# Windowed attention and an ELU feed-forward network in fp32 on one core: softmax spread over the blocks around it, one PSUM copy moved to VectorE, masks between transposes

## The chip, the cores and the metric

One core of one Trainium2 chip. The metric is the device time of one execution in microseconds. The core has TensorE (PE; PEld is its weight load), VectorE (DVE), ScalarE (ACT), GpSimd (POOL) and SyncE (SP, which issues the transfers here).

## The reference

```python
def _attn_ref(q, k, v):              # 8 batches, 8 heads, 576 positions, 64 wide
    scores = np.matmul(q, k.transpose(0, 1, 3, 2)) / np.sqrt(D)
    rel = pos[:, None] - pos[None, :]
    mask_plain = (rel >= 0) & (rel < 32)                      # heads 0 to 3
    mask_dil = (rel >= 0) & (rel < 128) & (rel % 4 == 0)      # heads 4 to 7
    scores = np.where(masks, scores, -1e9)
    scores = scores - scores.max(-1)
    attn = np.exp(scores); attn = attn / (attn.sum(-1) + 1e-9)
    return np.matmul(attn, v)

def _moe_ref(x, w_in, w_out):        # x: 4608 x 512, w_in: 512 x 2048, w_out: 2048 x 512
    h = x @ w_in
    g = np.where(h > 0, h, np.exp(np.minimum(h, 0)) - 1)
    return g @ w_out
```

The attention's result, with the heads side by side, is the x of the feed-forward network.

## The kernel before

The 4608 tokens are cut into 9 chunks of 512, the 8 batches have 576 tokens each. The attention of batch b has to be ready before the chunks that hold its tokens, so it is done in pieces between the matmuls of earlier chunks. Matmuls in fp32 accuracy are made of three passes over a rounded value (`h`, `gh`, `xh`: a cast on ScalarE) and its residual (`l`, `gl`, `xl`: a subtraction on VectorE).

**Chunks 0 to 2** loop over 16 blocks `f` of 128 hidden columns. A block is one first product (12 matmuls of 512 columns), the ELU (`elu`: ScalarE copies the PSUM tile, exponential, relu; VectorE combines; ScalarE casts `gh`; VectorE subtracts `gl`), and the second product of the block two before it (`flush`, 12 matmuls of 512 columns). `elu` is a generator: its tail, cast and `gl`, is run within the next block's `elu`, after that one's copy of the PSUM tile. In chunk 2's last blocks the tail runs at once. In chunks 1 and 2 weight blocks are also split (`split_late`, L180 and L182) and combined for the later chunks (`combine`, L230 to L237, in the blocks that `COMBINE` names).

**Chunks 3 to 8** (`combined_chunk`) replace the first product of 2 x 2 blocks by seven products of sums of blocks (`ORDER`), in four groups `g` of seven steps `s`. Each step is a product (12 matmuls of 256 columns), then what `TODO[s]` lists for ScalarE and VectorE, operand casts and residuals (`moving_operand`, listed in `OPERANDS`; `rest:B22` is the residual of operand B22), and some second products from a queue (`pop`). `work(spare)`, the entries `w0` to `w6`, takes softmax steps from the list `side` up to a budget of `SPARE[g][s]`.

**The attention pieces.** A scores piece (`scores_piece`, two head pairs, 144 small matmuls) uses three PSUM banks: the two `a_ps` and `h1`, shown as `h`. After a third of it, a one-column copy into `nothing` (L481) reads the third bank, so that the last third of the matmuls, which writes this bank for the second head, comes after it. Then the masks are added from PSUM into `sm` (VectorE), maximum, subtraction, exponential (ScalarE), sum, normalisation and six 32-row transposes into `pt`, for each head pair. An output piece (`outputs_piece`, 48 matmuls) needs both pairs' transposes. For batches 2 and 3 (`b <= CS`), the scores pieces stand in chunk 1, blocks 0 and 7, and in chunk 2, blocks 1 and 7, the output pieces in blocks 6 and 13 and in blocks 6 and 12 (`WHEN`), and all of the softmax is written right after the scores. For batches 4 to 7 `later_probabilities` adds the masks at once and puts the rest on `side`; batch 4's first piece stands in chunk 2, block 14, the others in chunks 3 to 6, at steps 9 and 23 of the 28 (`PIECES`). There are two `sm` buffers: a tile `sm` and a part of `a5` (shown as `a`). At step 9 the list `side` is emptied before the piece (`work(100.0)`).

**What sets the order.** All matmuls, and every operation given to `vec` and `act`, are pinned: each stands on its engine's queue behind the operation that was written before it. Other operations of VectorE and ScalarE (`nc.vector`, `nc.scalar`) are ordered by a planner, which runs the program in a simulated time and takes what is ready, the earlier written first. In chunks 1 and 2 the ELU and softmax are of this kind, until chunk 2's block 14 (`LAST`), from where all are pinned.

Of the kernel before, what the change touches and what calls it, by code (L numbers as in the profile page):

```python
# [24 lines left out]
G = 32  # L25
# [18 lines left out]
CS = 3  # L44
# [7 lines left out]
SPARE = ((0.9, 0.3, 1.0, 0.9, 1.2, 2.2, 0.3), (0.9, 0.9, 0.0, 1.6, 2.2, 1.0, 0.3), (0.9, 0.9, 2.2, 1.2, 2.0, 2.4, 0.3), (0.6, 0.6, 0.0, 0.3, 0.6, 1.2, 0.3))  # L52
OPERANDS = [t.split() for t in ("", "cast:B11 make:T1", "rest:B11", "make:T2 cast:T2", "rest:T2", "make:T3", "cast:T3 rest:T3",
                                "cast:B21 rest:B21", "make:T4 cast:T1", "rest:T1 cast:T4", "rest:T4 cast:B22", "rest:B22", "", "")]
WHEN = {1: (0, 6, 7, 13), 2: (1, 6, 7, 12)}
EARLY = 0.0
LAST = 14
OPER = 12
PLAIN = ("a5", "a-1'")
COMBINE = {(1, 11): 0, (1, 13): 1, (1, 15): 2, (2, 1): 3, (2, 4): 4, (2, 6): 5, (2, 9): 6, (2, 11): 7}  # L60
PIECES = {9: ("S", 2, 1), 14: ("O", 0, 1), 21: ("O", 2, 1), 23: ("S", 0, 2)}

TINY = float(np.array([0x38000000], np.uint32).view(np.float32)[0])
# [3 lines left out]
def body(ctx: ExitStack, tc: tile.TileContext, q, k, v, masks, w_in, w_out, out):  # L67
# [235 lines left out]
    def normalise(eng, sm, sums, keep):  # L303
        keep(nc.vector.tensor_scalar(out=sums, in0=sums, scalar1=1e-9, scalar2=None, op0=ALU.add))
        keep(nc.vector.reciprocal(out=sums, in_=sums))
        return keep(eng.tensor_tensor(out=sm, in0=sm, in1=sums.unsqueeze(2).broadcast_to([QB, 2 * NU, 2 * G]), op=ALU.mult))

    def transposed():
        count[0] += 1
        return pt[count[0] % len(pt)]  # L310
# [89 lines left out]
    def probabilities(b, hp, sm, nmx, sums):  # L400
# [10 lines left out]
                last_transpose[b] = nc.vector.transpose(out=tr[ks, :, cs], in_=sm[cs, :, rs]).ins  # L411
        return b, hp, tr

    def three():

        return banks() + [ps_h.tile([P, TC], F32, name="h1")]
# [9 lines left out]
    vec, act = Ordered(nc.vector), Ordered(nc.scalar)  # L426
    side, held = [], []

    def work(spare):

        while side and spare > 0:
            cost, step = side.pop(0)
            step()
            spare -= cost

    def later_probabilities(b, hps, groups):

        other_sm = slots("a5", 2, 3).rearrange("p o t -> p (o t)")[:QB, :2 * NU * 2 * G].rearrange("p (u j) -> p u j", u=2 * NU)
        sms = [ap.tile([QB, 2 * NU, 2 * G], F32, name="sm", bufs=1), other_sm]
        for j in (1, 0):  # L440
            masks_added(hps[j], groups[j], sms[j], vec)
        small = [[ap.tile([QB, 2 * NU], F32, name=n, bufs=4) for n in ("nmx", "sums")] for _ in hps]
        trs = [transposed() for _ in hps]
        wide = lambda x: x.unsqueeze(2).broadcast_to([QB, 2 * NU, 2 * G])

        def steps(j):

            sm, (mx, sums), tr = sms[j], small[j], trs[j]
            yield 0.9, lambda: vec.tensor_reduce(out=mx, in_=sm, op=ALU.max, axis=mybir.AxisListType.X)
            yield 0.9, lambda: vec.tensor_tensor(out=sm, in0=sm, in1=wide(mx), op=ALU.subtract)  # L450
            yield 0.0, lambda: act.activation(out=sm, in_=sm, func=AF.Exp, scale=0.125)
            yield 0.9, lambda: vec.tensor_reduce(out=sums, in_=sm, op=ALU.add, axis=mybir.AxisListType.X)
            yield 0.1, lambda: vec.tensor_scalar(out=sums, in0=sums, scalar1=1e-9, scalar2=None, op0=ALU.add)
            yield 0.1, lambda: vec.reciprocal(out=sums, in_=sums)
            yield 0.9, lambda: vec.tensor_tensor(out=sm, in0=sm, in1=wide(sums), op=ALU.mult)
            for c in range(GU):
                for r in range(2):
                    ks, cs, rs = slice((c + r) * G, (c + r + 1) * G), slice(c * G, (c + 1) * G), slice(r * G, (r + 1) * G)
                    yield 0.57, lambda ks=ks, cs=cs, rs=rs: vec.transpose(out=tr[ks, :, cs], in_=sm[cs, :, rs])

        one, other = list(steps(0)), list(steps(1))
        side.extend([*one[:2], other[0], one[2], other[1], one[3], other[2], *one[4:7], *other[3:7]])
        (held if hps[0] else side).extend(one[7:] + other[7:])
        return [(b, hp, tr) for hp, tr in zip(hps, trs)]

    def scores_piece(b, hps):

        s = three()

        def place(j, h, n0, n1):  # L470

            bank, o = (s[h], n0 + j * NU) if j == 0 or n0 < 2 else (s[2], n0 - 2 + h * 4)
            return bank[:, o * 2 * G:(o + n1 - n0) * 2 * G]

        qk = [qk_of.pop(b * NPAIR + hp) for hp in hps]

        one, other = [(0, n) for n in range(NU)], [(1, n) for n in range(NU)]
        for i, (first_head, second_head) in enumerate(zip(other[2:] + other[:2] + one, other[:2] + one + other[2:])):
            if i == 4:

                nc.scalar.copy(out=nothing, in_=place(1, 0, NU - 1, NU)[:QB, 2 * G - 1:])  # L481
            for c in range(GU):
                for h, (j, n) in enumerate((first_head, second_head)):
                    score(place(j, h, n, n + 1), *qk[j], h, n, c)
        groups = [[[(n0, n1, place(j, h, n0, n1)) for n0, n1 in (((0, NU),), ((2, NU), (0, 2)))[j]] for h in range(2)] for j in range(2)]
        if b <= CS:
            made = [probabilities(*exponentials(b, hp, groups[j])) for j, hp in enumerate(hps)]
        else:
            made = later_probabilities(b, hps, groups)
        for hp in hps:  # L490
            load_qk(b * NPAIR + hp + 2)
        return made
# [238 lines left out]
    def combined_chunk(c):  # L731

        x_ps = y_ps = None
        halves = lambda x: x.rearrange("p (i t) -> p i t", i=2)
        for g in range(NG):
            base = (c - CS) * NG * 7 + g * 7
            for s in range(7):
                step = 7 * g + s
                what, hp, ahead = PIECES.get(step, ("", 0, B))
                if what and c + ahead < B:  # L740
                    if what == "S":
                        if hp:
                            work(100.0)
                        made[hp] = scores_piece(c + ahead, (hp, hp + 1))
                    else:
                        if hp:
                            work(100.0)
                        outputs_piece(made.pop(hp))
                        if hp == 0:
                            side.extend(held)  # L750
                            held.clear()
                load_combined(base + s + RING)
                if s == 0:
                    x_ps = ps_h.tile([P, TC], F32, name="h0")
                    live["before"], live["now"] = live.get("now"), (c, g, [sets.pop(0), sets.pop(0)])
                    sets.extend(live["now"][2])
                if (c, g, s) == (CS, 1, 0):
                    moving["temporary"] = late
                if s == 3:
                    y_ps = ps_h.tile([P, TC], F32, name="h1")  # L760
                product(base + s, x_ps if ORDER[s] in ("A11", "S2", "S3", "A22") else y_ps, s in (0, 3, 4))
                for what in TODO[s]:
                    if what in ("u1", "u2", "u3"):
                        live[what] = fp.tile([P, TC], F32, name="e")
                        act.copy(out=live[what], in_=x_ps)
                    elif what == "C21":
                        act.copy(out=rows[1][:, :, :HT], in_=halves(x_ps))
                    elif what[0] == "C":
                        to, u = {"C11": (rows[0][:, :, :HT], "u1"), "C22": (rows[1][:, :, HT:], "u3"), "C12": (rows[0][:, :, HT:], "u2")}[what]
                        vec.tensor_tensor(out=to, in0=halves(y_ps), in1=halves(live.pop(u)), op=ALU.add)  # L770
                    elif what[0] == "w":
                        work(SPARE[g][s])
                    elif what[0] == "p":
                        push(int(what[4:]))
                    else:
                        activation(what)
                if g == NG - 1 and c + 1 < NCH:
                    for what in OPERANDS[s]:
                        moving_operand(c + 1, what, vec, act)
                if g == 0:  # L780
                    for what in OPERANDS[7 + s]:
                        moving_operand(c, what, vec, act)
                pop((FIRST_POPS if (c, g) == (CS, 0) else POPS)[s])
# [83 lines left out]
    for c in range(CS):  # L867
# [14 lines left out]
        for f in range(NF):  # L882
# [29 lines left out]
            else:  # L912
                steps = elu(gemm1(c, f), c, f, before, *strict)
                g = next(steps)
                if c == 0 or c == CS - 1 and f >= NF - 3:
                    if g[1] is not None:
                        next(steps)
                    steps = None
                before = steps
                pend.append((c, f, g))  # L920
            if c == 1:
                keep_plain(f)
            if (c, f) == (0, 0):
# [103 lines left out]
```

## Time and profile before

| | |
|---|---|
| median of 3 runs | 884.86 us (884.64 to 887.34) |
| profiled execution | 884.33 us, span 882.5 us |
| TensorE clock granted, mean | 0.994 |
| PE busy | 863.4 us, 98% of the span |
| VectorE busy | 609.1 us, 69% |
| ScalarE busy | 455.7 us, 52% |
| chunk 2 (230 to 328 us) | VectorE busy 80.04 of 98.00 us |
| DMA | 170.68 MB, mean 193 GB/s |

The span runs from the first to the last instruction. In rows of the timeline the first number is the start in us from the span's beginning, the second the length, then engine, line, operation, output and inputs, shapes and count, and in brackets the engine's idle time before it and what ended that. The line is that of a helper for many: L104 is every matmul, L424 every pinned operation. In the list of waits, the numbers are total us, times, and the longest.

### The profile page before, as it was taken

What the parts mean: (1) busy time and instruction counts of PE and PEld (TensorE: products, weight loads), DVE (VectorE), ACT (ScalarE), POOL (GpSimd) and SP (SyncE); (2) the same over time, 40 slices, a digit from 0 to 9 for tenths busy, and PEclk for the clock granted to TensorE, in tenths of its full rate; (3) what the DMA queues carried; (4) which work ended last, traced back from release to release, by engine and by line L of the source; (5) the groups of instructions that cost most, each with busy time, mean ns of one, the idle gap of its engine ahead of it and who ended that gap; (6) DMA issues with size and microseconds to landing.
All of it is one profiled execution on the core that took longest, in us unless ns stands there. A gap on an engine that the chain in (4) does not pass through costs nothing. (4 is left out here: it accounts for less than half of the span.)

```text
span 882.5 us, 17850 instructions
## 1 busy us (share of the span) xinstructions
PE 863.4 (98%) x7424; PEld 725.6 (82%) x7424; DVE 609.1 (69%) x921; ACT 455.7 (52%) x783; POOL 6.0 (1%) x12
## 2 busy tenths in 40 slices
PE   6999999999999999999999999999999999999998
PEld 5545678878878888898989998889898989998996
DVE  6999998867588968966867597748775533453332
ACT  3666667645655565434554455446454453454334
POOL 2000000000000000000000000000000000000000
PEclk7999999999999999999999999999999999999999
DMA  9996335123454657757575657656665565557541
GB/s 342 387 356 245 123 121 187 48 92 120 155 199 156 198 165 226 227 187 236 176 258 188 225 178 248 219 182 223 196 199 167 167 215 176 183 175 224 175 144 48
DMA packets 66961, 170.68 MB, mean 193 GB/s; under 512 B 6752, under 2 KB 21440, under 8 KB 66880
## 3 DMA queue, kind: packets, MB, share of 16 engines
q1 hardware_dynamic: 66880, 169.54, 58.9%
q8 instruction: 59, 0.97, 0.4%
q14 instruction: 22, 0.18, 0.1%
HBM read 141.20 MB, written 28.31 MB: 192 GB/s over the span
## 5 line engine op out<-in xcount | busy, mean ns | idle before, releaser
L104 PE MATMUL h<-xh,r 128*128 128x256 f32 (+1 forms) x984 | 223.2, 308 | 2.1 <-PE h L104 1.0
L104 PEld LDWEIGHTS h<-xh,r 128*128 128x128 f32 x984 | 165.1, 191 | 13.9 <-PE h L104 1.2
L104 PE MATMUL h<-xl,r 128*128 128x256 f32 (+1 forms) x492 | 142.7, 307 | 0.6 <-DVE xl L424 0.6
L104 PE MATMUL o_ps<-a,r 128*128 128x512 f32 x480 | 117.0, 391 | 0.0
L424 DVE SCALAR_TENSOR_TENSOR a-1_3249<-a-1_3249,a 128x1024 f32<-128x1024 f32 x48 | 58.7, 1223 | 83.2 <-ACT a L424 83.1
L424 DVE TENSOR_TENSOR a-1_3249<-h,e 128x512 f32<-128x512 f32 x72 | 49.7, 690 | 82.5 <-PE h L104 81.1
L104 PEld LDWEIGHTS h<-xl,r 128*128 128x128 f32 x492 | 93.8, 191 | 9.0 <-issue 2.1
L104 PEld LDWEIGHTS o_ps<-a,r 128*128 128x128 f32 x480 | 87.6, 188 | 16.5
L104 PE MATMUL o_ps<-a,gh 128*128 128x512 f32 x248 | 89.4, 463 | 0.0
L424 ACT COPY e<-h 128x512 f32<-128x512 f32 x72 | 42.2, 586 | 80.8 <-PE h L104 65.7
L104 PE MATMUL h<-a,r 128*128 128x256 f32 x576 | 77.5, 284 | 0.0
L104 PEld LDWEIGHTS h<-a,r 128*128 128x128 f32 x576 | 74.0, 191 | 3.0
L424 ACT COPY a-1_3249<-h 128x512 f32<-128x512 f32 x24 | 14.1, 587 | 109.6 <-PE h L104 109.6
L104 PEld LDWEIGHTS o_ps<-a,gh 128*128 128x128 f32 x248 | 46.3, 188 | 24.2 <-issue 17.2
L424 ACT ACTIVATE a<-a 128x1024 f32<-128x1024 f32 (+1 forms) x56 | 57.0, 1030 | 1.3
L104 PE MATMUL o_ps<-r,r 128*128 128x512 f32 x212 | 56.8, 391 | 0.0
L104 PE MATMUL o_ps<-a,a 128*128 128x512 f32 x216 | 54.6, 391 | 0.0
L424 ACT ACTIVATE a<-a-1_3249 128x1024 f32<-128x1024 f32 x48 | 51.0, 1063 | 1.3 <-DVE a-1_3249 L424 0.5
L104 PEld LDWEIGHTS o_ps<-a,a 128*128 128x128 f32 x216 | 39.4, 188 | 7.4
L424 ACT CAST r<-a-1_3249 128x1024 fp32r<-128x1024 f32 x32 | 33.6, 1050 | 22.2 <-DVE a-1_3249 L424 22.1
L104 PEld LDWEIGHTS o_ps<-r,r 128*128 128x128 f32 x212 | 38.7, 188 | 7.3
L424 DVE TENSOR_TENSOR r<-a-1_3249,r 128x1024 fp32r<-128x1024 f32 x32 | 39.0, 1218 | 6.7 <-ACT r L424 6.2
(179 smaller groups left out, 1431.6 us busy)
## 6 DMA issues: line engine op xcount, KB each, us to landing
r<-combined SPq DMA_DIRECT2D x168, 512.0 KB, 4.1
vt<-v SPq DMA_DIRECT2D x30, 384.0 KB, 4.2
kt<-k SPq DMA_DIRECT2D x30, 304.0 KB, 4.9
out<-e SPq DMA_DIRECT2D x35, 256.0 KB, 3.1
qt<-q SPq DMA_DIRECT2D x30, 288.0 KB, 4.0
r<-w_in SPq DMA_DIRECT2D x16, 512.0 KB, 7.6
r<-w_out SPq DMA_DIRECT2D x16, 512.0 KB, 8.0
combined<-a SPq DMA_DIRECT2D x20, 256.0 KB, 2.9
```

The lines of the kernel that those rows point to most:

```text
L104: return inorder(nc.tensor.matmul(*args, **kw))
L424: return lambda *args, **kw: inorder(getattr(self.eng, name)(*args, **kw))
```

## The change

Six edits:

1. The first scores piece of chunk 2 goes from block 1 to block 2; its output piece stays in block 6.
2. For batches 2 and 3 the softmax is a generator, `softmax`. The first head pair's masks to normalisation are written at the scores; then, one entry of `spread` in each of the next four blocks, right after the block's ELU: three transposes of the first pair; its other three, and the second pair's masks to normalisation; three transposes of the second pair; its last three.
3. In blocks that hold an attention piece (`f in when`), the tail of this block's ELU (cast and `gl`) is written at once, ahead of the piece.
4. For batches 4 to 7 the one-column copy is a pinned VectorE operation.
5. In chunk 3, step 9, `work(100.0, LEFT)` leaves three transposes on `side`. `later_probabilities` then swaps the two `sm` buffers, adds the second pair's masks, does the three transposes, adds the first pair's masks, and lets the second pair go first in the steps that follow. With an empty list the order is the one before.
6. In chunk 3, group 0, step 4, `rest:B22` is written ahead of the step's list.

```diff
-WHEN = {1: (0, 6, 7, 13), 2: (1, 6, 7, 12)}
+WHEN = {1: (0, 6, 7, 13), 2: (2, 6, 7, 12)}
+LEFT = 3
...
+    spread = []
+    def softmax(b, hp, places, tr):
+        _, _, sm, _, sums = exponentials(b, hp, places)
+        normalise(nc.vector, sm, sums, lambda ins: ins)
+        yield
+        for c in range(GU):
+            for r in range(2):
+                ks, cs, rs = slice((c + r) * G, (c + r + 1) * G), slice(c * G, (c + 1) * G), slice(r * G, (r + 1) * G)
+                last_transpose[b] = nc.vector.transpose(out=tr[ks, :, cs], in_=sm[cs, :, rs]).ins
+                if (c, r) == (1, 0):
+                    yield
+        yield
...
-    def work(spare):
-        while side and spare > 0:
+    def work(spare, left=0):
+        while len(side) > left and spare > 0:
...
@@ later_probabilities @@
-        for j in (1, 0):
-            masks_added(hps[j], groups[j], sms[j], vec)
+        one, other = (1, 0) if side else (0, 1)
+        if side:
+            sms.reverse()
+        masks_added(hps[1], groups[1], sms[1], vec)
+        work(100.0)
+        masks_added(hps[0], groups[0], sms[0], vec)
...
-        one, other = list(steps(0)), list(steps(1))
+        one, other = list(steps(one)), list(steps(other))
...
@@ scores_piece @@
-                nc.scalar.copy(out=nothing, in_=place(1, 0, NU - 1, NU)[:QB, 2 * G - 1:])
+                (vec.tensor_copy if b > CS else nc.scalar.copy)(out=nothing, in_=place(1, 0, NU - 1, NU)[:QB, 2 * G - 1:])
...
-            made = [probabilities(*exponentials(b, hp, groups[j])) for j, hp in enumerate(hps)]
+            trs = [transposed() for _ in hps]
+            made = [(b, hp, tr) for hp, tr in zip(hps, trs)]
+            one, other = [softmax(b, hp, groups[j], trs[j]) for j, hp in enumerate(hps)]
+            next(one)
+            spread.extend(((one,), (one, other), (other,), (other,)))
...
@@ combined_chunk @@
-                            work(100.0)
+                            work(100.0, LEFT if c == CS else 0)
...
+                if (c, g, s) == (CS, 0, 4):
+                    moving_operand(c, *OPERANDS[7 + s], vec, act)
...
-                if g == 0:
+                if g == 0 and (c, s) != (CS, 4):
...
@@ the loop over blocks @@
+                if steps is not None and f in when:
+                    next(steps)
+                    steps = None
                 before = steps
                 pend.append((c, f, g))
+            for steps in spread.pop(0) if spread else ():
+                next(steps)
```

## Prediction

> **What bounds the kernel now.** I read the page first, then the waits of PE, then stretches of the timeline around each wait, engine by engine.
>
> ```profile
> span 882.5 us, 17850 instructions
> PE 863.4 (98%) x7424; PEld 725.6 (82%) x7424; DVE 609.1 (69%) x921; ACT 455.7 (52%) x783; POOL 6.0 (1%) x12
> ...
> q8 instruction: 59, 0.97, 0.4%
> ...
> PE h L104 <- issue: 0.9, 1, 0.9
> ```
>
> PE is busy 98% and the change alters no matmul. So only PE's holes can be won, and any new wait of PE is lost one for one. I price a hole by starts: from the last matmul before it to the first after it, less the usual distance (0.23 us at 512 columns, 0.12 at 256). The last line, from the list of PE's waits, is one in which it waits for nothing that the profile shows. Seven holes after 130 us are over 0.4 us. The change reaches all of them, and opens others.
>
> **The change part by part.** *Softmax of chunks 1 and 2 in pieces.* In the kernel before, both head pairs' softmax is written where the scores are, so in the written order it stands ahead of the residual `gl` of the block before:
>
> ```profile
> 183.87 0.69 DVE L573 SCALAR_TENSOR_TENSOR e<-h,e 128x512 f32<-128x512 f32 x1 [0.42 <-ACT e L572]
> 184.37 0.15 ACT L481 COPY nothing<-h 96x1 f32<-96x1 f32 x1 [0.54 <-PE h L104]
> 191.21 3.48 DVE L411 STREAM_TRANSPOSE pt<-sm 32x384 f32<-32x384 f32 x6
> 194.73 0.69 DVE L578 TENSOR_TENSOR gl<-e,gh 128x512 fp32r<-128x512 f32 x1
> 193.56 0.61 PE L104 MATMUL o_ps<-a,gh 128*128 128x512 f32 x2
> 195.47 0.50 PE L104 MATMUL o_ps<-a,gl 128*128 128x512 f32 x1 [1.29 <-DVE gl L578]
> ```
>
> `gl` could have followed the activation of 183.87; it ran 10 us later, behind six transposes. The second matmul of the pair began at 193.56 + 0.61 - 0.39 = 193.78, so the hole is 195.47 - 193.78 - 0.23 = **1.46**. The edit writes `gl` ahead of the scores and halves the transposes: I take the whole 1.46 as won (between 1.0 and 1.46; a block of three transposes, 1.74 us, is the longest it can still meet).
>
> *The piece of chunk 2 goes from block 1 to block 2.* Soon after the scores at 243.9 PE stops in the middle of a product for which nothing is outstanding:
>
> ```profile
> 243.90 0.24 PE L104 MATMUL h<-kt,qt 64*32 64x64 f32 x1
> ...
> 245.63 0.50 PE L104 MATMUL h<-xh,r 128*128 128x512 f32 x1
> ...
> 246.89 0.40 PE L104 MATMUL h<-xl,r 128*128 128x512 f32 x1
> 248.24 0.39 PE L104 MATMUL h<-xh,r 128*128 128x512 f32 x1 [0.95 <-issue]
> ...
> 248.53 1.18 ACT L236 CAST e<-a 128x512 fp32r<-128x512 f32 x2 [1.80 <-DMA out<-e]
> 249.80 0.59 ACT L558 COPY h<-h 128x512 f32<-128x512 f32 x1
> 249.18 1.29 DVE L237 TENSOR_TENSOR a<-a,e 128x512 fp32r<-128x512 f32 x2 [3.24 <-ACT e L236]
> 250.39 0.55 DVE L375 TENSOR_TENSOR sm<-a_ps,masks_sb 96x384 f32<-96x384 f32 x1
> ```
>
> That hole is 1.35 - 0.23 = **1.12**. The page's instruction queue moved 59 packets of 0.97 MB together, 16.4 KB each, for PE's 7424 matmuls and as many weight loads: some 252 instructions a packet. A scores piece is 144 matmuls with 144 loads in 245.63 - 243.90 = 1.7 us, more than one packet, so I read the stop as PE waiting for instructions. One block later the piece begins 48 instructions (24 matmuls and loads) further on against the packets, and of the eleven other pieces, which begin elsewhere against them, none is followed by such a row. I take the 1.12 as won (0 to 1.12). [...]
>
> The same rows show what the piece moves into. ScalarE is held until 248.53 by the stores of chunk 0's and 1's results. The copy of block 2's hidden tile comes at 249.80, and behind it a cast, an exponential and a relu of about 0.6 each (that copy's and the casts' time): to 252.1. The scores now begin one block later, 243.9 + 24 x 0.227 = 249.35, and their last third, 0.6 long, needs ScalarE's one-column copy (`nothing`) at 249.35 + 1.7 - 0.6 = 250.4. If that copy queues behind the three, PE waits 1.7; if it also queues behind the cast of block 2, which is now written ahead of the scores, 3.0; if the planner slips it in, 0. I take **1.3** lost (0 to 3.0), nearer to the first, since what is written first and ready goes first.
>
> *The outputs of that piece keep their place (block 6), so softmax has one block less.*
>
> ```profile
> 269.86 3.48 DVE L411 STREAM_TRANSPOSE pt<-sm 32x384 f32<-32x384 f32 x6
> 273.37 1.29 DVE L237 TENSOR_TENSOR a<-a,e 128x512 fp32r<-128x512 f32 x2
> 274.58 1.29 DVE L573 SCALAR_TENSOR_TENSOR e<-h,e 128x512 f32<-128x512 f32 x2
> ...
> 274.52 0.39 PE L104 MATMUL a_ps<-pt,vt 128*64 128x96 f32 x4
> ```
>
> VectorE needed 250.39 to 273.34, 22.95 us, from the second half of the first mask add to the last transpose; the outputs began 1.2 us after. With the change the masks start at the end of the scores, 250.9, with both halves to do (0.5 more): 250.9 + 0.5 + 22.95 = 274.35 at best. The outputs begin at 274.52 - 1.12 = 273.4 and come to the second pair's transposes halfway, at 274.35. But the last three transposes are now written at block 6, behind the two L237, the activation of block 5 and its `gl` (each 1.29 for two): 1.2 + 0.6 + 0.6 = 2.4 us more, and perhaps block 6's own pair, 1.2. Lost 0 to 3.6; the wait at 250.4 would let VectorE do some of this meanwhile. I take **2.0**.
>
> *Cast and `gl` ahead of the other pieces, and smaller holes under 0.2.* At 184.37 the copy ran before the cast was ready (the activation ended at 184.56); with the cast first it would end at 184.56 + 0.6 + 0.15 = 185.3 instead of 184.5, a little after which PE needs it. Net **0.2** lost (0 to 0.8).
>
> *The one-column copy goes from ScalarE to VectorE for batches 4 to 7*, pinned behind what VectorE was given before it. In chunks 4 and 6:
>
> ```profile
> 448.99 0.49 PE L104 MATMUL a_ps<-kt,qt 64*32 64x64 f32 x26
> 450.39 0.24 PE L104 MATMUL h<-kt,qt 64*32 64x64 f32 x1 [0.92 <-ACT nothing L481]
> 451.22 0.75 DVE L424 TENSOR_TENSOR a<-h,masks_sb 96x256 f32<-96x256 f32 x2 [4.36 <-PE h L104]
> 635.82 0.24 PE L104 MATMUL h<-kt,qt 64*32 64x64 f32 x1 [0.40 <-ACT nothing L481]
> ```
>
> Holes: 450.39 - (448.99 + 0.49 - 0.22) = **1.13**, 0.21 over the idle time that the row gives, and so 0.40 + 0.21 = **0.61** in chunk 6. VectorE sits idle there (4.36 before the masks), so both go. No row shows this copy on VectorE; between 0 and the 0.37 of one mask add (two in 0.75) I take 0.15, ScalarE's own time for it (184.37). It is done in time with either.
>
> But batch 4's first piece stands in chunk 2's block 14, where every operation is pinned:
>
> ```profile
> 322.66 0.46 PE L104 MATMUL a_ps<-kt,qt 64*32 64x64 f32 x23
> 323.35 0.24 PE L104 MATMUL h<-kt,qt 64*32 64x64 f32 x1 [0.23 <-ACT nothing L481]
> 323.94 0.69 DVE L424 SCALAR_TENSOR_TENSOR e<-h,e 128x512 f32<-128x512 f32 x1 [2.29 <-ACT e L424]
> 325.32 0.69 DVE L424 TENSOR_TENSOR r<-e,gh 128x512 fp32r<-128x512 f32 x1 [0.69 <-ACT gh L424]
> 325.93 0.74 DVE L424 TENSOR_TENSOR a<-h,masks_sb 96x256 f32<-96x256 f32 x2
> ```
>
> There VectorE waits for the relu, then for the cast, and the mask adds come only at 325.93. The copy now stands right ahead of them: 325.93 + 0.15 and 0.05 to PE's start, and PE goes on at 326.13 instead of 323.35. That is **2.78 lost**, where a free VectorE would have won the 0.45 of this hole (323.35 less 322.66 + 0.46 - 0.24, and the piece's own step). No later slack takes it back: the next hidden product follows on PE, and the VectorE operations after the masks wait for that product in turn. Ends: 2.6 and 3.0 by the price of the copy.
>
> *Chunk 3: `rest:B22` first, masks between the transposes.*
>
> ```profile
> 340.46 0.69 DVE L424 TENSOR_TENSOR a-1_3249<-h,e 128x512 f32<-128x512 f32 x1 [0.68 <-PE h L104]
> 343.26 0.68 DVE L424 TENSOR_TENSOR xl<-x,xh 128x512 fp32r<-128x512 f32 x1
> 343.08 0.28 PE L104 MATMUL h<-xh,r 128*128 128x256 f32 x1
> 343.99 0.39 PE L104 MATMUL h<-xl,r 128*128 128x256 f32 x1 [0.63 <-DVE xl L424]
> 354.39 3.48 DVE L424 STREAM_TRANSPOSE pt<-a 32x384 f32<-32x384 f32 x6
> 358.00 0.75 DVE L424 TENSOR_TENSOR a<-h,masks_sb 96x256 f32<-96x256 f32 x2
> 356.15 1.70 PE L104 MATMUL h<-r,r 128*128 128x256 f32 x12
> 358.86 0.36 PE L104 MATMUL h<-xh,r 128*128 128x256 f32 x1 [1.01 <-PE h L104]
> ```
>
> The residual of 343.26 moves ahead of 340.46, into 0.68 us of idle time: hole 343.99 - 343.08 - 0.12 = **0.79** gone. The second hole, 358.86 - (356.15 + 1.70 - 0.28) - 0.12 = **1.17**, is PE waiting for the bank `h` that the two mask adds of 358.00 release; they stand behind seven transposes of 0.58, one and the six of 354.39. Three now come after: the adds could start 1.7 us earlier. But the copy on VectorE also stands behind the four that stay: 354.39 + 3 x 0.58 = 356.13, where PE wants it for the last third of the scores, 0.6 before the product of 356.15, at 355.55 less the 0.79 just won. So a new wait of up to 1.5 opens inside the scores, 0.8 if VectorE's chain, which starts from PE's results, moves up by 0.7 with PE. Of 0.79 + 1.17 = 1.96 I take 1.96 - 0.85 = **1.1** won (0.45 to 1.96).
>
> **The sum.** Won: 1.46 + 1.12 + 1.13 + 0.61 + 1.1 = 5.42. Lost: 2.78 + 1.3 + 2.0 + 0.2 = 6.28. Net +0.86 on the profiled execution's 884.33 (span 882.5 and 1.8 around it): 885.2. The median of the runs, 884.86, is 0.53 above that execution, so **885.7** in their terms. What a measurement can tell from no change is about 0.3%, 2.65 us: 882.2 to 887.5.
>
> **The rivals.** *The planner lets the early pieces through.* ScalarE's copy at block 2 goes ahead of the backlog and the transposes run before L237: 1.3 + 2.0 + 0.2 not lost, 885.7 - 3.5 = 882.2. For it: VectorE and ScalarE outside pinned stretches are ordered by readiness (the L237 pair at 249.18 cut between two halves of a mask add). Against: where several were ready at once, as from 273.37 on, they ran in written order. Chance 0.18; half of it beyond 0.3%.
>
> *The copy at block 14 is not held* (it would have to run before the `gl` of 325.32): 885.7 - 2.78 - 0.45 = 882.5. Only a wrong reading of the pinning allows it. Chance 0.08.
>
> *Slower: the cast ahead of the one-column copy on ScalarE.* At all four pieces of chunks 1 and 2 the cast now stands first in written order.
>
> ```profile
> 141.93 0.69 DVE L573 SCALAR_TENSOR_TENSOR e<-h,e 128x512 f32<-128x512 f32 x1 [0.39 <-ACT nothing L481]
> ```
>
> At block 0 of chunk 1 the copy would end at 141.93 + 0.69 + 0.6 + 0.15 = 143.4 instead of 141.9: 1.5. Block 7 costs 0.6, block 2 of chunk 2 3.0, its last piece some 0.2: 5.3 where the sum has 1.5, so 889.5. It decides the sign when the four pass 3.3 together. For it: written order won from 273.37 on. Against: at 184.37 the copy was ready first. Chance 0.22.
>
> *The stop at 246.89 is no fetch and stays:* 886.8, within the band; chance 0.1, which I leave in the forecast's.
>
> **How the numbers follow.** The forecast has 0.52, the rivals 0.18, 0.08 and 0.22. Faster by over 0.3%: 0.09 + 0.05 and a little for both of the first two together: 0.16. Slower: 0.22 and 0.04 from the forecast's upper end: 0.26. The rest, 0.58, is within. The forecast's own range is 883.0 to 888.0; for 8 in 10 it goes from 881.8 (first rival, a little beyond) to 888.8 (most of the third).
>
> **What would show it.** No wait of PE for L578 `gl` near 194; no issue gap after the scores of chunk 2; a wait of PE near 323 of about 3.2 us, for VectorE's `nothing`; no wait for `xl` near 343, and near 355 one for `nothing` instead of 1.0 before 358.86; none near 449 and 635. The unsure ones: PE for ScalarE's `nothing` near 250, and for `pt` near 274. I am wrong if the piece at block 14 runs through, or if those two are near 0 or near their upper ends.

## Result and profile after

The changed kernel takes 892.79 us (median, 891.02 to 894.61) against 885.69 (884.64 to 887.34) for the kernel before in the same runs: a ratio of 1.0081, 95% interval 1.0064 to 1.0098. It is 7.1 us slower; the forecast was 885.7 in a range of 881.8 to 888.8. The profiled execution took 892.01 us, 7.68 more than the one of before (884.33).

From the page of the kernel after, and the top of PE's list of waits from 130 us on (total, times, longest):

```profile
span 890.2 us, 17851 instructions
PE 865.8 (97%) x7424; PEld 726.6 (82%) x7424; DVE 611.9 (69%) x929; ACT 455.4 (51%) x775; POOL 6.0 (1%) x12
...
PE h L105 <- DVE nothing L440: 4.4, 2, 3.0
PE h L105 <- ACT nothing L501: 2.3, 2, 1.5
PE h L105 <- ACT h L582: 1.5, 1, 1.5
PE o_ps L105 <- DVE gl L602: 0.7, 1, 0.7
PE a_ps L105 <- DVE pt L425: 0.6, 1, 0.6
```

The first, second and fifth were in the prediction. The fourth is not the wait for `gl` that was to go, but one for the `gl` of the next block. The third was not foreseen: PE waits for ScalarE's copy of a hidden tile out of its bank `h`. These are its rows (ScalarE, then VectorE, then PE):

```profile
141.96 0.62 ACT L601 CAST gh<-e 128x512 fp32r<-128x512 f32 x1
148.51 0.84 ACT L397 ACTIVATE sm<-sm 96x768 f32<-96x768 f32 x1 [4.03 <-DVE sm L396]
149.26 0.56 ACT L582 COPY h<-h 128x512 f32<-128x512 f32 x1
...
142.62 0.69 DVE L602 TENSOR_TENSOR gl<-e,gh 128x512 fp32r<-128x512 f32 x1 [0.69 <-ACT gh L601]
143.22 0.55 DVE L376 TENSOR_TENSOR sm<-a_ps,masks_sb 96x384 f32<-96x384 f32 x1
143.69 2.35 DVE L183 TENSOR_TENSOR a<-a,a 128x1024 fp32r<-128x1024 f32 x2
145.96 0.55 DVE L376 TENSOR_TENSOR sm<-a_ps,masks_sb 96x384 f32<-96x384 f32 x1
...
148.00 0.39 PE L105 MATMUL o_ps<-r,gl 128*128 128x512 f32 x1
149.88 0.50 PE L105 MATMUL h<-xh,r 128*128 128x512 f32 x1 [1.49 <-ACT h L582]
```

The cast and `gl` run ahead of the mask adds. Between PE's scores and the second mask add now stand `gl` (0.60 us) and two adds of L183 (2.27 us), which split a weight block. In the kernel before the same two adds run at 140.32 and 152.86. They are tied to `gl` in the code: `split_late` stands under `issue_after(low[-1])` and `issue_after(high[-1])`, behind the last `gl` and cast that were written. With the tail of block 0 written at once, that is block 0's for both, so one add is held back until then and the other is let go early; that is read from the code, and the times of both kernels fit it. ScalarE's exponential therefore gets its operand at 148.49. The copy of `h` stands behind it on ScalarE's queue and does not pass it, though ScalarE idles for 4.03 us and the last matmul of the product to be copied began before 145.5. In the kernel before, the same exponential had run 3 us earlier, at 145.55, the copy at 146.31, and PE went on without a hole:

```profile
145.55 0.85 ACT L396 ACTIVATE sm<-sm 96x768 f32<-96x768 f32 x1 [3.62 <-DVE sm L395]
146.31 0.57 ACT L558 COPY h<-h 128x512 f32<-128x512 f32 x1
...
148.22 0.39 PE L104 MATMUL h<-xh,r 128*128 128x512 f32 x1
```

The hole, by starts, is 149.88 - 148.00 - 0.23 = 1.65 us. At block 14 of chunk 2 (VectorE's rows), and then in the busy time by stretches (PE, PEld, VectorE, ScalarE, GpSimd, then the granted clock):

```profile
328.39 0.69 DVE L440 SCALAR_TENSOR_TENSOR e<-h,e 128x512 f32<-128x512 f32 x1 [2.29 <-ACT e L440]
329.77 0.69 DVE L440 TENSOR_TENSOR r<-e,gh 128x512 fp32r<-128x512 f32 x1 [0.68 <-ACT gh L440]
330.38 0.15 DVE L440 COPY nothing<-h 96x1 f32<-96x1 f32 x1
...
318.00:325.00 7.00, 7.00 (x33) 5.80 (x32) 5.17 (x13) 5.10 (x12) 0.00 (x0) 1.00 0.61 198
329.50:336.30 6.80, 5.72 (x57) 4.59 (x58) 2.83 (x8) 0.23 (x1) 0.00 (x0) 0.50 0.48 157
336.30:343.00 6.70, 6.70 (x42) 5.96 (x42) 3.54 (x6) 4.13 (x9) 0.00 (x0) 1.00 0.31 100
```

The copy stands where the prediction put it, right behind the `gl` of that block. It takes 0.15 us, as estimated. PE's hole is 3.22 us; the one of before was 0.44, so the hold costs 2.78. What was not foreseen is the second row of the stretches: with the hold, TensorE drops to half clock for 6.83 us. The scores of block 14 began 4.44 us later than before, those of chunk 3 8.85 us. Of the 4.41 between them, 2.78 are the hold and 0.79 the `xl` hole, won back; 2.42 are left over, which I put down to the half clock.

The other pieces. Around 195 and 201 the order of VectorE and what PE does, at block 2 of chunk 2 the order of ScalarE, and near 364 that of VectorE again:

```profile
185.84 0.69 DVE L602 TENSOR_TENSOR gl<-e,gh 128x512 fp32r<-128x512 f32 x1 [0.68 <-PE h L105]
195.84 0.39 PE L105 MATMUL o_ps<-a,gl 128*128 128x512 f32 x1
...
194.29 3.48 DVE L425 STREAM_TRANSPOSE pt<-sm 32x384 f32<-32x384 f32 x6
197.81 0.69 DVE L597 SCALAR_TENSOR_TENSOR e<-h,e 128x512 f32<-128x512 f32 x1
201.45 0.68 DVE L602 TENSOR_TENSOR gl<-e,gh 128x512 fp32r<-128x512 f32 x1
202.19 0.50 PE L105 MATMUL o_ps<-a,gl 128*128 128x512 f32 x1 [0.75 <-DVE gl L602]
...
253.03 0.62 ACT L601 CAST gh<-e 128x512 fp32r<-128x512 f32 x1 [0.76 <-DVE e L597]
253.56 0.15 ACT L501 COPY nothing<-h 96x1 f32<-96x1 f32 x1
...
363.46 0.57 DVE L440 STREAM_TRANSPOSE pt<-sm 32x384 f32<-32x384 f32 x1
364.06 1.73 DVE L440 STREAM_TRANSPOSE pt<-a 32x384 f32<-32x384 f32 x3
365.82 0.15 DVE L440 COPY nothing<-h 96x1 f32<-96x1 f32 x1
```

The `gl` that had stopped PE at 193.8 in the kernel before ran at 185.84, and the matmul that reads it ran at 195.84 without a hole. But the six transposes, written in halves, still ran as one block of 3.48 us, ahead of the next block's activation (197.81), though its relu had ended at 193.62. That block's `gl` came only at 201.45, behind the transposes and the mask adds, maximum and subtraction of the other head pair: a new hole of 0.91. At block 2 the one-column copy ran behind the cast, as in the prediction's upper case; here that cost 1.67 us. Near 364 it ran behind four transposes: 1.61 us.

### The profile page after: what moved, and what is told of

It reads as the page before. It is cut to its first block, busy times and chain, and to the rows that moved or that the text cites. A ratio compares the mean times of both kernels' runs of the same rounds, so it can differ in the third digit from the quotient of the medians.

```text
span 890.2 us, 17851 instructions
## 1 busy us (share of the span) xinstructions
PE 865.8 (97%) x7424; PEld 726.6 (82%) x7424; DVE 611.9 (69%) x929; ACT 455.4 (51%) x775; POOL 6.0 (1%) x12
## 4 chain that ended last, share of the span: by engine, by line
PE 79%; DVE 12%; ACT 4%; issue 2%; DMA 1%; POOL 0%; SPq 0%; DVEq 0%; ACTq 0%
PE h L105 38%; PE o_ps L105 37%; PE a_ps L105 4%; DVE pt L425 2%; DMA out<-e 1%; DVE nmx L389 1%; DVE sm L376 1%; DVE e L597 1%; DVE sm L307 1%; DVE gl L602 1%; DVE sm L396 1%; DVE a L183 0%; ACT pt L362 0%; DMA kt<-k 0%; DVE sums L398 0%
```

## Experiments

Each median is beside that of the kernel before in runs on the same chip: 885.2 us for the first four, 884.97 for the next four, 884.36 for the last four. Holes are start to start, less the usual distance, as in the prediction.

**One part undone, one part alone: the copy at block 14.** First from the kernel after, then from the kernel before.

```diff
-                (vec.tensor_copy if b > CS else nc.scalar.copy)(...)
+                (vec.tensor_copy if b > CS and (b > CS + 1 or hps[0] > 0) else nc.scalar.copy)(...)
```

> The changed kernel, with the one-column copy of batch 4's first piece (chunk 2, block 14) back on ScalarE and nothing else undone. Theory A: the hold of 3.2 us there costs 2.8 us itself and, by setting the granted clock to one half for 6.8 us behind it, about 2.4 us more. Then this run takes 892.8 - 5.2 = 887.6, the products after the piece start 0.23 us apart and the mean granted clock is near 0.995. Rival B: the half clock has nothing to do with the hold. Then 890.0, with the clock still near 0.992.

Measured 889.17 us, ratio 1.0041 (1.0027 to 1.0055), 3.5 us below the kernel after (0.0081 - 0.0041 of 885). That lies between the two figures expected, and fits neither. The hold at block 14 is gone. But in its profiled execution ScalarE's copy at block 2 held PE for 3.49 us instead of 1.67, and 3.41 us of half clock followed there.

```diff
-                nc.scalar.copy(...)
+                (vec.tensor_copy if b == CS + 1 and hps[0] == 0 else nc.scalar.copy)(...)
```

> The kernel before, with only the one-column copy of batch 4's first piece moved to VectorE, behind what VectorE holds there. Theory A: 885.7 + 2.8 + 2.4 = 890.9, with a stretch of half clock behind the piece. Rival B: 888.5 at an undisturbed clock. Rival C: something later takes the hold back, 886 or less.

Measured 888.52 us, ratio 1.0039 (1.0026 to 1.0053): 3.3 us lost by one copy of 0.15 us. Its hole is 3.22 us, as in the kernel after. Here the profile shows full clock behind it:

```profile
PE h L105 <- DVE nothing L440: 3.0, 1, 3.0
...
326.50:333.30 6.80, 6.80 (x79) 5.89 (x80) 2.77 (x7) 2.34 (x4) 0.00 (x0) 1.00 0.53 178
```

**The late edits alone, and the early edits alone.** The first is the kernel before with only what concerns batches 5 to 7 and chunk 3: the copy on VectorE for `b > CS + 1`, mask adds between transposes, `rest:B22` first. The second has only the edits of chunks 1 and 2: the piece at block 2, softmax spread, cast and `gl` ahead; all copies stay on ScalarE.

> The kernel before, with the edits of chunks 3 to 6 alone: rest:B22 early, masks between transposes at chunk 3's step 9, the copy on VectorE for batches 5 to 7 only (batch 4 keeps it on ScalarE). Theory A: the four holes close, 0.79 + 1.17 + 1.13 + 0.61 = 3.7, so 882.0. Rival B: VectorE's chain is the next limit in chunk 3, so the 0.79 and 1.17 come back as another wait there; 884.0.

Measured 882.95 us, ratio 0.9972 (0.9960 to 0.9983): faster than both kernels. The holes at 343, 449 and 635 are gone. In place of the 1.17 us at 357.6 there is one of 1.06, with no releaser, shown below; so the gain is between the two figures expected.

> The kernel before, with the edits of chunks 1 and 2 alone: softmax in pieces, the scores piece in block 2, cast and residual ahead of the pieces; the copy stays on ScalarE everywhere, chunk 3 as before. Theory A: the waits that the changed kernel's trace shows before chunk 2's block 14 are due to these edits, net 4.1 us at that point (326.34 - 321.90 less 0.3 that the two runs differ at the start): 889.8. Rival B: as predicted for these terms, 1.46 + 1.12 won, 3.5 lost: 886.6.

Measured 890.41 us, ratio 1.0059 (1.0040 to 1.0077). So the early edits, priced at 3.5 lost against 2.58 won, lose 5.2 us, close to theory A. In this profile the wait for ScalarE's copies is the longest, 3.53 us by starts at block 2:

```profile
PE h L105 <- ACT nothing L501: 4.1, 2, 3.3
...
252.54 0.63 ACT L587 ACTIVATE e<-h 128x512 f32<-128x512 f32 x1 [2.12 <-DMA out<-e]
```

The second row shows why it is longer here than in the kernel after: ahead of the cast and the copy, ScalarE's exponential waits 2.12 us for a store of results (2.09 in the profile with 3.49 us), where it waits 0.17 in the profile of the kernel after.

**The three early edits, each alone.**

```diff
-WHEN = {1: (0, 6, 7, 13), 2: (1, 6, 7, 12)}
+WHEN = {1: (0, 6, 7, 13), 2: (2, 6, 7, 12)}
```

> The kernel before with only the first scores piece of chunk 2 put at block 2 instead of block 1. By the prediction's terms the stop of 1.12 us at 246.9 goes and ScalarE's copy `nothing` costs 1.3 us: 885.2 + 0.2 = 885.4 us. Rival, from the profile after: the copy waits behind the exponential and the cast of gh, PE holds for 1.67 us (3.5 us where the copy is the later one), and the stop of 1.12 us came in only some executions, so that nothing is won by losing it: 886.9 to 888.7 us.

Measured 885.64 us, ratio 1.0009 (1.0000 to 1.0018): close to no change. That is near the 885.4 expected, but by other terms: the copy is not held by itself (its hole at block 2 is 0.22 us), no stop follows the scores, and the outputs wait 1.43 us at 275.

> The kernel before with only the probabilities of the pieces of chunks 1 and 2 spread over the blocks that follow. By the prediction's terms the hole of 1.45 us at 193.8 goes and 0.2 us is lost to casts: 885.2 - 1.3 = 883.9 us. Rival, from the profile after: the hole keeps 0.91 us, PE waits 1.65 us at 148 for ScalarE's copy of h that is queued behind the exponential, and 0.3 to 1.0 us each at 186, 215 and 286: 885.2 - 0.54 + 1.65 + 0.29 + 0.31 + 1.01 = 887.9 us.

Its edit is the one of `scores_piece` in the diff above (`softmax`, `spread`). Measured 884.30 us, ratio 0.9994 (0.9985 to 1.0004): no change that can be told. No hole at 148; 0.87 us are left of the one at 194, so the median is near the 883.9 expected without the gain that was to bring it there.

```diff
+                if steps is not None and f in when:
+                    next(steps)
+                    steps = None
```

> The kernel before with only the second output step put one block earlier where a scores piece stands. The prediction's 2.0 us came from transposes that are spread; without the spread they are over when the outputs begin, so no change: 885.2 us, within 0.6. Rival: the outputs wait for pt as they do in the profile after (0.22 and 0.80 us), whether the transposes are spread or not: 886.2 us.

That text names the edit wrongly: what these lines move is the cast to `gh` and `gl` of a block, ahead of the piece, and no output step. Both its prices fall. Measured 889.22 us, ratio 1.0040 (1.0027 to 1.0053): this edit alone loses 4.25 us. Its waits between 130 and 300 us:

```profile
PE o_ps L105 <- DVE gl L598: 2.7, 2, 1.9
PE h L105 <- ACT h L578: 1.5, 1, 1.5
PE h L105 <- issue: 1.2, 1, 1.2
```

The hole at 148 (1.68 us) comes with it. The `gl` that it was to bring forward is in time, and the 1.45 us at 194 are gone; but those of the next two blocks are late, by 0.92 at 201 and 2.06 at 207. The profiled execution, 886.60 us, is the second fastest of the ten (885.63 to 890.96) and only 2.3 us above that of the kernel before; what the slower ones lose besides, no profile shows.

**Is a stop without a releaser a wait for code?** The late edits again, with all later instructions of PE 76 places further on:

```diff
+        for _ in range(38 if hp == 0 else 0):
+            mm(s_ps[:, 0, 0:8], ones_sb, mask_sb[:, 0, 0:8], start=True, stop=True)
         for h in range(2):
             mm(s_ps[:, h, :], ones_sb, mask_sb[:, int(dil), :], start=True, stop=False)
```

> The kernel of the late edits alone (882.95 us) with 38 small products more ahead of TensorE's first scores, in the time in which it waits for its first operands, so that every later instruction of TensorE stands 76 places later against its packets of code. If the stop of 1.06 us at 357.6 is a wait for code, it goes, and the time is 881.9 us. Rival: it is a wait for data; the profile shows it at the same product, and the time stays at 882.9 us. A wait for code can also come up at another piece, which then begins 130 to 150 instructions into its packet as the pieces with stops do; the profile shows where.

Measured 885.46 us, ratio 1.0005 (0.9996 to 1.0014), neither figure: 2.3 us are lost at the start already. The stop moved. From the kernel of the late edits (first two rows) and from this one:

```profile
357.64 0.28 PE L105 MATMUL h<-xh,r 128*128 128x256 f32 x1
358.82 0.28 PE L105 MATMUL h<-xl,r 128*128 128x256 f32 x1 [0.89 <-issue]
...
635.78 1.70 PE L105 MATMUL h<-r,r 128*128 128x256 f32 x12
639.31 0.39 PE L105 MATMUL h<-xh,r 128*128 128x256 f32 x1 [1.83 <-issue]
```

The instruction queue moved 59 packets for PE's 15067 matmuls, weight loads and semaphore instructions, some 255 each. Counted in blocks of 256 (an estimate: 59 packets of 255 would hold 15045, too few), the scores that the first stop follows begin at place 134. Shifted, those begin at 210 and run through, while the scores at 634, now at 136, are followed by a stop of 1.99 us. In these two profiles it goes with the place in the code, not with the data. The place alone does not suffice: two other shifted pieces, at 125 and 132, are followed by none. In the trace's packets of the instruction queue one lands from 356.52 to 357.48 and PE goes on at 358.82; in the shifted kernel one lands from 636.94 to 637.88 and PE goes on at 639.31. In both PE goes on 1.3 to 1.4 us after a packet of code has come, which is what a wait for code would look like.

The small products also changed VectorE's order, 190 us later (first two rows the late edits, then this kernel):

```profile
192.15 3.48 DVE L412 STREAM_TRANSPOSE pt<-sm 32x384 f32<-32x384 f32 x6
195.66 0.69 DVE L598 TENSOR_TENSOR gl<-e,gh 128x512 fp32r<-128x512 f32 x1
...
193.10 0.69 DVE L600 TENSOR_TENSOR gl<-e,gh 128x512 fp32r<-128x512 f32 x1
196.12 3.47 DVE L414 STREAM_TRANSPOSE pt<-sm 32x384 f32<-32x384 f32 x6
```

No edit touched that place; the hole of 1.44 us there went, and one at 261 grew from 0.71 to 1.62.

**The kernel after, without cast and `gl` ahead.**

> The kernel after with one part undone: at the pieces of chunks 1 and 2 the cast to gh and the residual gl of the block stand behind the scores again, as before; all else as after. (This is the edit whose run alone gave 889.2 us; what moves in it is the cast and gl, not an output step.) If that edit is what the prediction had too small, the time is 892.6 - 4.2 = 888.4 us, and PE's wait of 1.5 us for ScalarE's copy of h near 148 is gone, while the hold of 3.2 us at block 14 stays. Rival: the loss lies in the edits meeting each other; then the time stays at 891 or more.

Measured 887.19 us, ratio 1.0033 (1.0021 to 1.0046), against 1.0081: 4.2 us less, as much as the edit alone loses. The wait for the copy of `h` is gone, the hold at block 14 stays:

```profile
PE h L105 <- DVE nothing L440: 4.4, 2, 3.0
PE a_ps L105 <- DVE pt L425: 1.7, 1, 1.7
```

**Cast and `gl` ahead at one place of eight,** block 0 of chunk 1 (`(c, f) == (1, 0)` for `f in when`), from the kernel before.

> The kernel before with the cast to gh and gl ahead of the scores at one place of eight, block 0 of chunk 1. If the hole of 1.65 us at 148 comes from there (the mask adds fall behind gl and the two adds of 1.2 us each, the exponential behind them, and ScalarE's copy of h is queued behind the exponential): 885.0 + 1.65 = 886.6 us and the hole at 148. Rival: it comes from the order of the whole plan, and one place alone does not bring it: 885.0 us.

Measured 886.13 us, ratio 1.0015 (1.0006 to 1.0023): 1.77 us, and the hole (1.71 us) is there with the same queue on ScalarE:

```profile
149.23 0.84 ACT L397 ACTIVATE sm<-sm 96x768 f32<-96x768 f32 x1 [4.02 <-DVE sm L396]
149.98 0.56 ACT L578 COPY h<-h 128x512 f32<-128x512 f32 x1
150.59 0.50 PE L105 MATMUL h<-xh,r 128*128 128x512 f32 x1 [1.55 <-ACT h L578]
```

**A longer hold.** The copy at block 14 on VectorE, 26 times instead of once.

> The kernel with only batch 4's first copy on VectorE (888.5 us, hold of 3.2 us), with 25 more of the same copies behind it, some 0.15 us each, that PE's next scores wait for too: a hold of about 7 us. If a long enough hold brings half clock, every execution shows it behind this hold, 3.4 us or more of it: 888.5 + 3.8 + 1.7 or more = 894 us or more. Rival: the half clock after the hold of 3.2 us in the kernel after had another cause: 892.3 us and full clock.

Measured 894.29 us, ratio 1.0106 (1.0086 to 1.0125). All four executions have a mean clock of 0.990 to 0.992, below all 23 of the kernel before beside it (0.993 to 0.999). That fits, but does not prove it for the three without a profile: the mean also holds a stretch of half clock in the first 28 us (10.24 us in the profile of the kernel before, 6.83 in that of the kernel after), and the shifted kernel, without such a hold but with 13.65 us of it there in its profile, has 0.991 or 0.992 in six of its eleven. In the profile the hold is 7.93 us and the half clock 6.83:

```profile
327.90:334.70 6.80, 3.71 (x52) 2.99 (x53) 4.56 (x23) 0.00 (x0) 0.00 (x0) 0.50 0.22 71
334.70:341.00 6.30, 6.30 (x37) 5.49 (x36) 2.03 (x3) 3.57 (x7) 0.00 (x0) 0.99 0.48 146
```

**A better version.** The late edits with the spread softmax.

> The late edits (882.95 us) and the spread softmax of chunks 1 and 2 (0.7 us below the kernel before by itself); piece of chunk 2 at block 1, cast and gl behind the scores, batch 4's first piece with its copy on ScalarE. If the parts add: 885.0 - 2.2 - 0.7 = 882.1 us. Rival: the spread is worth nothing, its 0.7 us being within its interval: 882.8 us.

Measured 880.98 us, ratio 0.9958 (0.9945 to 0.9971). It beats both kernels and is the fastest of these, though its interval meets that of the late edits alone and the two profiled executions are alike (881.86 and 881.88 us, on two chips). That the spread adds something to the late edits is not shown.

## Why the prediction was wrong

The sum's own terms, against holes of the two profiled executions (us):

| term | predicted | measured |
|---|---|---|
| won: `gl` at 193.8 | 1.46 | 1.46 |
| won: stop at 246.9 | 1.12 | 1.12 |
| won: `nothing` at 449 and 635 | 1.74 | 1.74 |
| won: chunk 3, net | 1.1 | 0.0 (1.96 gone; 1.61 and 0.34 new) |
| lost: copy at block 14 | 2.78 | 2.78 |
| lost: its half clock | none | 2.42 (what is left over) |
| lost: `nothing` at block 2 | 1.3 | 1.67 |
| lost: outputs waiting for `pt` | 2.0 | 0.80 |
| lost: cast and `gl` ahead of other pieces | 0.2 | 3.86 (1.65, 0.29, 0.91, 1.01) |
| lost: holes under 0.6 elsewhere, net | none | 0.68 |
| net lost | 0.86 | 7.9 (7.68 by the times) |

*Right:* the hold at block 14, by its place, mechanism and size, from rows that show VectorE waiting for the relu and the cast (shown by undoing it and by doing it alone); the `gl` at 193.8, in time once it stands ahead of the scores; and the recovery at 449 and 635, where the holes are gone in the kernel after and with the late edits alone. They are no fixed price, though: in the profiles of the kernels that keep this copy on ScalarE the waits for it from 440 to 650 us come to 0.7 to 2.1 us, 1.4 on average.

*The step that failed first: "Cast and `gl` ahead of the other pieces", taken at 0.2 with an upper end of 0.8.* By the medians it loses 4.25 us alone and 4.2 in company. The step followed only one ScalarE copy, at one piece (184.37). It did not ask what comes later on VectorE once `gl` stands first (the mask adds), who waits for that (the exponential), and what is queued behind *that* (the copy of `h`, which PE waits for). Most of the delay at block 0 comes from the two adds that are tied to `gl` (2.27 us, with 0.60 for `gl` itself).

The third rival, slower with 889.5, had the right edit and nearly the size. Its mechanism, the one-column copy behind the cast, acts at three of its four pieces: 0.29 us at block 7, 1.67 at block 2 of chunk 2 and 1.01 at the last piece, against 0.6, 3.0 and 0.2. At block 0, where it said 1.5, the copy ran first (141.77, the cast at 141.96), and the hole of 1.65 is the other chain; that this nearly equals 1.5 is luck. At block 2 the moved piece is cheap only without the other edit: alone the copy is held 0.22 us, with the cast ahead as well 1.67, 3.49 and 3.53 in three profiles. The three early edits together lose 5.2 us and the sum of each alone is 4.25 (4.25 + 0.7 - 0.7); that goes the same way, but the difference lies within the intervals.

*The second: the hold was priced as its own length.* "Lost one for one" took full clock for granted. Half clock followed the hold at block 14 in the profiles of the kernel after and of the long hold, and not in two others with the same 3.22 us. For executions without a profile there is only the mean clock, which fits a half clock that comes in some executions and does not show it. The six of the kernel after have 0.989 to 0.996 and spans of 892.7 to 889.2 us. The kernel without cast and `gl` ahead spans 883.6 to 884.8 us in its three executions at 0.998, 884.6 to 888.2 in its eight at 0.994 or less, and 887.5 in one at 0.996.

*The third: "a block of three transposes, 1.74 us, is the longest it can still meet".* The planner decided anew and kept the six transposes in one block, ahead of an activation that was written before them and ready. The next block's `gl` paid for it, with 0.91 in the kernel after and 0.92 with cast and `gl` ahead alone. With the spread alone five of the six ran ahead of the first `gl`, and 0.87 of its 1.45 us remain. Shown is that edits far away change this order (38 small products at the start); by what estimate it is chosen was not tried.

*Mis-sized:* chunk 3's net. The copy behind four transposes costs 1.61 where 0.85 was taken and 1.5 was the bound: VectorE's chain did not move up with PE. Alone, with this copy on ScalarE, the late edits give 2.25 us of the 3.70 of their four rows (0.79, 1.17, 1.13, 0.61); the stop of 1.06 us at 357.6 takes most of the difference. The mask adds are out of the way there, and PE's stop without a releaser is about as long as the 1.17 us that it had waited for them. The outputs' 2.0 was more than twice too much.

*The stop at 246.9.* What the runs show fits the reading, a wait for code, without proving it: the stop goes when the piece or the code is moved, and it ends 1.22 us after a packet of the instruction queue (245.64 to 247.02). But it isn't a fixed price. Where the piece stands at block 1 and no later code is shifted, the profiles show it at 1.12, under 0.22, 0.23, 0.93, 1.36, 1.11, 0.54 and 0.52 us, 0.75 on average, and PE goes on 1.1 to 1.6 us after such a packet in all eight. Nor do the other pieces all begin elsewhere, as the prediction says: this one begins at place 148 of its block of 256 (counted as above), those at 354.6 and 404.3 at 134 and 132, and the kernel before has no such row behind them. The kernel before has 59 packets of the instruction queue, 50 of them from 130 us on, and one such stop in that time, behind the 288 instructions of a scores piece in 1.7 us.

## What to carry over

Moving an operation ahead on one engine is priced by following everything that it pushes back, through the next engine's queue (here the copy of `h` did not pass the exponential, though ScalarE idled for 4.03 us), to the first instruction there that TensorE needs, even if that has nothing to do with the operation moved. What is tied to the moved operation moves too. Where a planner sets the order, being written earlier is only a hint, and each edit may reorder places that it doesn't touch; read the order of the built kernel, and test every part alone. A hold of TensorE of about 3 us may cost its length nearly twice: 2.78 and 2.42 us more here, in one profile.

## What the runs showed of the hardware

In the traces of both kernels the clock's changes lie on a grid of 3.413 us. In that of the kernel before, the stretches of one clock last 3.413, 10.24 (half clock, to 22.59) and 860.16 us: 1, 3 and 252 times 3.4133. In that of the kernel after they last 3.413, 6.827 (half clock, to 22.30), 307.20, 6.827 (half clock, from 329.50) and 552.96 us: 1, 2, 90, 2 and 162 times.

How the hold lies on that grid went with what followed it. PE's idle time inside one stretch of the grid was 1.93, 2.86 and 3.41 us in the three profiles with half clock behind the hold (kernel after, copy at block 14 on ScalarE, long hold), and at most 1.77, 1.71 and 1.81 us in the three without (that copy alone, early edits, kernel after without cast and `gl` ahead), though those holds were 3.22 to 3.53 us long. No other stretch of the fourteen profiles between 25 and 875 us has over 1.7 us outside a half clock. A limit between 1.81 and 1.93 us would be an estimate from these six holds alone: in the first 25 us the kernel before has half clock behind a stretch (8.93 to 12.35) with 1.73 us. Behind the three holds half clock lasted 6.83, 3.41 and 6.83 us.

Extra products in PE's starting wait were not free: 38 of them, of 8 columns each, delayed the first scores of chunk 1 by 2.3 us. In the first 35 us the profile shows two waits without a releaser that the late edits' kernel doesn't have. They end at 13.49 and 21.11, 1.4 and 1.3 us after a packet of the instruction queue has come, so they too fit a wait for code:

```profile
PE a L105 <- issue: 1.9, 1, 1.9
PE b L105 <- issue: 1.6, 1, 1.6
```
